# Second-layer gate as one ScalarE function, and every feed-forward low half on VectorE

## The chip, the cores and the metric

One Trainium2 chip, one core. The metric is the time of one execution on the device, in microseconds (us); lower is better. The engines are named as the profile names them: PE (TensorE matmul), PEld (TensorE weight load), DVE (VectorE), ACT (ScalarE), POOL (GpSimd), SP (SyncE, here only a DMA queue).

## What is computed

A clustered attention, a feed-forward layer with squared ReLU, and a second feed-forward layer whose gate is `h * sigmoid(1.702 h)`. All in float32, 1536 tokens, model width 512, inner width 2048.

```python
def _moe_ref(x, w_in, w_out):
    h = np.maximum(x @ w_in, 0.0)
    return (h * h @ w_out).astype(np.float32)

def _moe2_ref(x, w_in, w_out):
    h = x @ w_in
    g = h * (1.0 / (1.0 + np.exp(-1.702 * h)))
    return (g @ w_out).astype(np.float32)

x = attention(q, k, v, centroids)     # masked by cluster, then reshaped to (1536, 512)
x = _moe_ref(x, **moe)
return _moe2_ref(x, **moe2)
```

## The kernel before

**Halves.** Each float32 operand of the feed-forward matmuls is held as two numbers in the matmul type fp32r: a high half (ACT copies and rounds it) and a low half (the operand minus its high half). A product is three matmul passes, high x high, low x high and high x low (`PASSES`). So every weight and every activation needs one ACT copy and one subtraction, and the matmuls wait for both.

**Stages in time.** Attention runs to about 250 us. Then come four feed-forward stages. In the first layer's hidden part (L671) a unit is 12 matmuls, 48 units. In the first output part (L841) a unit is again 12 matmuls: 32 units for two of the three token blocks (c = 0, 1), then 16 for c = 2. In the second layer's hidden part the weights are taken in pairs j = 0 to 7 of inner blocks; by a Strassen-like scheme, a pair takes seven products (P1 to P7, L705, six matmuls each) and two plain ones in two pieces (Q0, Q0, Q1, Q1, L714), 11 x 6 = 66 matmuls. The second output part (L841) is as the first.

**What feeds PE.** `w_stages` makes a weight from its float64 words: `magnitude` (L207, ACT), `clamp` (L210), `shift` (L214), `join_low` (L218), `join_high` (L222), all DVE, then `high` (L226, ACT) and `low` (L229, POOL). `g_high` (L824, ACT) and `g_low` (L828, DVE) halve the activations for the output parts. For the second hidden part, DVE adds token blocks (`t_sum`, L857) and ACT and POOL halve them (`moving_high` L863, `moving_low` L867); DVE adds weight blocks (`sums_of`, four instructions at L805) and ACT and POOL halve the sums (L808, L811). DVE and ACT copy banks out (L850).

**The gate.** A product's bank is finished in three ways. `take` (L730, ACT) copies a partial sum to memory, and the next product adds onto the same bank, so PE must wait for the copy: P6 waits for the take behind P1, P7 for the one behind P6, P3 for the one behind P5. `plus` (L733, DVE) adds the stored partial sum to the bank. The gate of a bank is `gate_banked` (L718, ACT, sigmoid) and `times_banked` (L721, DVE, product); that of a stored sum is `gate_stored` (L724, ACT) and `times_stored` (L727, POOL). In the last pair the sum stays in a bank.

**Order.** Nothing is scheduled by the compiler. Each step is put into one list by `at(key, f)`, sorted by key and issued in that order; each engine runs its own in order, and an instruction that waits holds everything behind it on its engine. A weight's seven steps are 0.25 apart in key units (one unit is 12 matmuls).

## Time and profile before

| what | us |
| --- | --- |
| median of 3 runs | 782.68 (782.37 to 782.76) |
| the profiled execution: its time | 782.82 |
| the profiled execution: span of the core | 780.8 |
| PE busy | 762.9 of 780.8 |
| DVE, ACT, POOL busy | 516.9, 444.8, 275.7 |
| granted TensorE clock | 1.00 throughout |

Busy time of an engine is read stretch by stretch, since the stages have different limits. A PE row with a bracket, as `[0.92 <-ACT arena L730]`, says that PE stood idle for 0.92 us before it and what ended the wait. The duration in a row runs from the start of an instruction to its end, whatever it did in between. The slice line of the page shows PE at 9 tenths or more in every slice but the first and the last, which stand at 8.

### The profile page before, as it was taken

To read this page: it belongs to the slowest core of one execution; us is meant where nothing else is said; L and a number is where in the kernel's file an instruction comes from. 1 tells how busy PE (TensorE), PEld (TensorE's weight loads), DVE (VectorE), ACT (ScalarE), POOL (GpSimd) and SP (SyncE) were. 2 spreads that over 40 slices of the span, in tenths; PEclk is the share of its full clock that TensorE was granted. 3 is DMA by queue.
4 is the path that set the end of the run, shared out by engine and by line. 5 is a ranking of instruction groups with operands and counts; after the bars stand their busy time and mean duration, and the time that the engine had idled before them with its cause. 6 is when DMAs were issued, how large, how long until landed. Compare 5 with 4: busy or idle time off the path is not lost.

```text
span 780.8 us, 10718 instructions
## 1 busy us (share of the span) xinstructions
PE 762.9 (98%) x3899; PEld 597.5 (77%) x3899; DVE 516.9 (66%) x854; ACT 444.8 (57%) x823; POOL 275.7 (35%) x209
## 2 busy tenths in 40 slices
PE   8999999999999999999999999999999999999998
PEld 5676676777777788888888887788777778888886
DVE  6787877877876444444487249865888888777321
ACT  7877778778766566666644224454554555443321
POOL 3665664664501122122122005643655641222000
PEclk9999999999999999999999999999999999999999
DMA  5132322322220122223133000100211222221201
GB/s 183 42 102 63 90 74 61 89 74 55 52 87 25 58 95 94 101 88 109 55 108 109 1 27 1 55 27 28 82 54 55 81 82 82 85 104 55 107 1 55
DMA packets 18197, 54.54 MB, mean 70 GB/s; under 512 B 2720, under 2 KB 2976, under 8 KB 18144
## 3 DMA queue, kind: packets, MB, share of 16 engines
q1 hardware_dynamic: 17856, 53.32, 21.5%
q8 instruction: 31, 0.51, 0.2%
q10 hardware_dynamic: 288, 0.52, 0.2%
q14 instruction: 22, 0.18, 0.1%
HBM read 43.02 MB, written 3.15 MB: 59 GB/s over the span
## 4 chain that ended last, share of the span: by engine, by line
PE 77%; DVE 14%; ACT 5%; issue 2%; POOL 0%; DMA 0%; DVEq 0%; ACTq 0%; POOLq 0%
PE bank L841 30%; PE bank L671 15%; PE ps_v L576 8%; PE ps_p L558 7%; PE ps_s L533 4%; PE ps_s L536 4%; DVE arena L805 3%; PE bank L705 2%; DVE arena L210 2%; DVE arena L218 2%; PE ps_h L671 1%; ACT arena L550 1%; PE bank L714 1%; DVE arena L857 1%; DVE arena L542 1%
## 5 line engine op out<-in xcount | busy, mean ns | idle before, releaser
L841 PE MATMUL bank<-arena 128*128 128x512 f32 x1152 | 262.5, 389 | 1.6 <-DVE arena L828 1.6
L841 PEld LDWEIGHTS bank<-arena 128*128 128x128 f32 x1152 | 216.0, 188 | 47.7 <-DVE arena L828 2.9
L229 POOL TENSOR_TENSOR arena<-arena,arena 128x512 fp32r<-128x512 f32 x64 | 82.9, 1296 | 275.8 <-ACT arena L226 232.5
L828 DVE TENSOR_TENSOR arena<-arena,arena 128x512 fp32r<-128x512 f32 x96 | 80.0, 839 | 85.8 <-ACT arena L824 83.2
L671 PE MATMUL bank<-arena 128*128 128x512 f32 x528 | 119.8, 389 | 0.0
L824 ACT CAST arena<-arena 128x512 fp32r<-128x512 f32 x96 | 59.5, 621 | 99.4 <-PE bank L841 99.2
L671 PEld LDWEIGHTS bank<-arena 128*128 128x128 f32 x528 | 99.1, 188 | 20.5
L542 DVE TENSOR_SCALAR_CACHE_REDUCE arena<-ps_s 128x768 bf16<-128x768 f32 x96 | 91.8, 956 | 33.8 <-PE ps_s L536 25.2
L550 ACT ACTIVATE arena<-ps_s,arena 128x768 f32<-128x768 f32 x96 | 87.1, 907 | 37.5 <-DVE arena L542 37.2
L210 DVE TENSOR_SCALAR arena<-arena 128x512 f32<-128x512 f32 x64 | 46.3, 724 | 71.9 <-ACT arena L207 71.9
L705 PE MATMUL bank<-arena 128*128 128x512 f32 x336 | 82.0, 392 | 6.3 <-ACT arena L730 5.5
L226 ACT CAST arena<-arena 128x512 fp32r<-128x512 f32 x64 | 39.7, 620 | 77.2 <-DVE arena L222 77.2
L705 PEld LDWEIGHTS bank<-arena 128*128 128x128 f32 x336 | 62.5, 188 | 22.0 <-ACT arena L730 8.0
L576 PE MATMUL ps_v<-arena 128*64 128x384 f32 x384 | 72.1, 498 | 0.0
L558 PE MATMUL ps_p<-arena 128*128 128x128 f32 x576 | 70.8, 272 | 0.0
L558 PEld LDWEIGHTS ps_p<-arena 128*128 128x128 f32 x576 | 65.7, 141 | 2.3 <-issue 0.6
L533 PE MATMUL ps_s<-arena 128*128 128x384 f32 x192 | 54.7, 366 | 2.4 <-ACT arena L550 2.3
L536 PE MATMUL ps_s<-arena 80*128 80x384 f32 x192 | 49.9, 341 | 0.1
L218 DVE SCALAR_TENSOR_TENSOR arena<-arena 128x512 int32<-128x512 int32 x64 | 47.4, 740 | 1.8
L714 PE MATMUL bank<-arena 128*128 128x512 f32 x192 | 48.1, 389 | 0.0
L222 DVE SCALAR_TENSOR_TENSOR arena<-arena 128x512 int32<-128x512 int32 x64 | 46.2, 721 | 1.9
L566 DVE COPY arena<-ps_p 128x512 f32<-128x512 f32 x72 | 46.9, 677 | 0.0
(111 smaller groups left out, 910.3 us busy)
## 6 DMA issues: line engine op xcount, KB each, us to landing
arena<-in_w_dram SPq DMA_DIRECT2D x64, 512.0 KB, 3.2
arena<-arena SPq DMA_DIRECT2D x32, 192.0 KB, 2.5
arena<-in_k_t_dram SPq DMA_DIRECT2D x8, 384.0 KB, 3.8
arena<-in_v_dram SPq DMA_DIRECT2D x8, 384.0 KB, 3.3
out_dram<-arena SPq DMA_DIRECT2D x11, 256.0 KB, 2.1
arena<-in_q_t_dram SPq DMA_DIRECT2D x7, 384.0 KB, 3.4
arena<-arena SPq DMA_DIRECT2D x28, 48.0 KB, 2.1
arena<-in_q_t_dram ACTq DMA_DIRECT2D x1, 384.0 KB, 3.5
```

The lines of the kernel that those rows point to most:

```text
L218: nc.vector.scalar_tensor_tensor(out=x[0], in0=words[:, :, 0], scalar=29, in1=x[0], op0=ALU.logical_shift_right, op1=ALU.bitwise_or)
L229: nc.gpsimd.tensor_tensor(out=halves[:, 1, :], in0=x[0].bitcast(F32), in1=halves[:, 0, :].bitcast(F32), op=ALU.subtract)
L533: nc.tensor.matmul(ps[:, n, :HALF], lhsT=x_s[i][:, t * P:(t + 1) * P], rhs=k1_s[i][:, n * HALF:(n + 1) * HALF], start=True, stop=False)
L536: nc.tensor.matmul(ps[:, n, :HALF], lhsT=q2_s[i][:, t * P:(t + 1) * P], rhs=k2_s[i][:, n * HALF:(n + 1) * HALF], start=False, stop=True)
L542: nc.vector.tensor_scalar(out=unused, in0=s_t[g][:, :, :HALF], scalar1=-scale, scalar2=None, op0=ALU.mult, op1=ALU.min, accum_out=m_t[g])
L550: nc.scalar.activation(out=p_t[g].rearrange("p (n f) -> p n f", n=2), in_=s_t.pop(g)[:, :, :HALF], func=AF.Exp, bias=m_t.pop(g), scale=sca ...
L558: nc.tensor.transpose(ps[:, x * P:(x + 1) * P], p_t[2 * k + j][:, t * P:(t + 1) * P], ident)
L576: nc.tensor.matmul(pv_t[n][j * D:(j + 1) * D, :HALF], lhsT=raw[n // 2, "v"][:, j, t, :], rhs=pt_t[n, j][:, t, :], start=(t == 0), stop=(t ...
L671: nc.tensor.matmul(ps, lhsT=w[:, a, kk * P:(kk + 1) * P], rhs=xf[:, b, kk, c * CH:(c + 1) * CH], start=(n == 0), stop=(n == 3 * KD - 1))
L705: nc.tensor.matmul(ps, lhsT=w[:, a, off + x * P:off + (x + 1) * P], rhs=MOVING[moving][x][:, b, :], start=(n == 0 and name in ("P1", "P2", ...
L828: nc.vector.tensor_tensor(out=t[:, 1, :], in0=g_t[m][:, c, :], in1=t[:, 0, :].bitcast(F32), op=ALU.subtract)
L841: nc.tensor.matmul(ps, lhsT=lhsT, rhs=rhs, start=(m == 0 and e == 0), stop=(m == MF - 1 and e == 2))
```

## The change

The second layer's gate becomes one ACT instruction, the function `Gelu_apprx_sigmoid` (the argument times the sigmoid of 1.702 times it), written in place for stored sums and out of the bank for the others; the 27 products on DVE (L721) and the 21 on POOL (L727) are gone, and the last pair's sums go to memory as in the other pairs. The low halves of weights (62 of 64: those of the first layer's hidden blocks 0 and 1, made during attention, stay on POOL), of weight sums (16) and of token blocks (14) go from POOL to DVE. Keys are as before.

```diff
         def low():
-            nc.gpsimd.tensor_tensor(out=halves[:, 1, :], in0=x[0].bitcast(F32), in1=halves[:, 0, :].bitcast(F32),
-                                    op=ALU.subtract)
+            (nc.gpsimd if layer == 0 and which == 0 and m < 2 else nc.vector).tensor_tensor(
+                out=halves[:, 1, :], in0=x[0].bitcast(F32), in1=halves[:, 0, :].bitcast(F32), op=ALU.subtract)
...
-            def gate_banked(ps, g):
-                nc.scalar.activation(out=g, in_=ps, func=AF.Sigmoid, scale=1.702)
-
-            def times_banked(ps, g):
-                nc.vector.tensor_tensor(out=g, in0=ps, in1=g, op=ALU.mult)
-
-            def gate_stored(t, g):
-                nc.scalar.activation(out=t, in_=g, func=AF.Sigmoid, scale=1.702)
-
-            def times_stored(t, g):
-                nc.gpsimd.tensor_tensor(out=g, in0=g, in1=t, op=ALU.mult)
+            def gate(x, g):
+
+                nc.scalar.activation(out=g, in_=x, func=AF.Gelu_apprx_sigmoid)
...
                     for name, ps, g in (("P2", c12, g00), ("P7", u_, g11), ("P3", c2x, g01)):
-                        if last:
...
-                        else:
-                            t = g_t[MF - 2 + gates[0] // 3 % 2][:, gates[0] % 3, :]
-                            gates[0] += 1
-                            after(name, j, 0.12, on(plus, ps, g, g))
-                            after(name, j, 0.7, gate_stored, t, g)
-                            after(name, j, 1.2, times_stored, t, g)
-                    after("P4", j, 0.1, on(gate_banked, u_, g10))
-                    after("P4", j, 0.6, on(times_banked, u_, g10))
+                        after(name, j, 0.12, on(plus, ps, g, g))
+                        after(name, j, 0.7, gate, g, g)
+                    after("P4", j, 0.1, on(gate, u_, g10))
...
                 def split_low(to, of):
-                    nc.gpsimd.tensor_tensor(out=to[:, 1, :], in0=of, in1=to[:, 0, :].bitcast(F32), op=ALU.subtract)
+                    nc.vector.tensor_tensor(out=to[:, 1, :], in0=of, in1=to[:, 0, :].bitcast(F32), op=ALU.subtract)
...
             def moving_low(name, x):
                 t = MOVING[name][x]
-                nc.gpsimd.tensor_tensor(out=t[:, 1, :], in0=moving_whole(name, x), in1=t[:, 0, :].bitcast(F32), op=ALU.subtract)
+                nc.vector.tensor_tensor(out=t[:, 1, :], in0=moving_whole(name, x), in1=t[:, 0, :].bitcast(F32), op=ALU.subtract)
```

In the changed file the lines behind the gate have moved: `plus` L733 is L725, `take` L730 is L722, the gate is L719, `sums_of` L805 and L811 are L781 and L787, `g_low` L828 is L804, `t_sum` L857 is L833, `moving_low` L867 is L843. The order of PE's and of ACT's instructions is otherwise unchanged (one gate stands where one sigmoid stood, and one table load before the first of them, as before); POOL's queue ends with attention's last step and the two lows that it keeps.

DVE in the second layer's hidden part, one middle pair, before: behind the two sums of one pair (banks 2632 and 2636) come the four weight sums, two products of gates, then a weight, a sum, a product, a weight.

```order
L733 TENSOR_TENSOR arena_59<-bank_2632,arena_59 128x512
L733 TENSOR_TENSOR arena_59<-bank_2636,arena_59 128x512
L805 TENSOR_TENSOR arena_59<-arena_59 128x256 x4
L721 TENSOR_TENSOR arena_59<-bank_2639,arena_59 128x512
L721 TENSOR_TENSOR arena_59<-bank_2632,arena_59 128x512
L210 TENSOR_SCALAR arena_59<-arena_59 128x512
L214 TENSOR_SCALAR arena_59<-arena_59 128x512
L218 SCALAR_TENSOR_TENSOR arena_59<-arena_59 128x512
L222 SCALAR_TENSOR_TENSOR arena_59<-arena_59 128x512
L733 TENSOR_TENSOR arena_59<-bank_2635,arena_59 128x512
L721 TENSOR_TENSOR arena_59<-bank_2638,arena_59 128x512
L210 TENSOR_SCALAR arena_59<-arena_59 128x512
```

The same place in the changed kernel:

```order
L725 TENSOR_TENSOR arena_59<-bank_2632,arena_59 128x512
L725 TENSOR_TENSOR arena_59<-bank_2636,arena_59 128x512
L781 TENSOR_TENSOR arena_59<-arena_59 128x256 x4
L787 TENSOR_TENSOR arena_58<-arena_59,arena_58 128x512
L210 TENSOR_SCALAR arena_59<-arena_59 128x512
L787 TENSOR_TENSOR arena_58<-arena_59,arena_58 128x512
L214 TENSOR_SCALAR arena_59<-arena_59 128x512
L218 SCALAR_TENSOR_TENSOR arena_59<-arena_59 128x512
L222 SCALAR_TENSOR_TENSOR arena_59<-arena_59 128x512
L725 TENSOR_TENSOR arena_59<-bank_2635,arena_59 128x512
L229 TENSOR_TENSOR arena_58<-arena_59,arena_58 128x512
L210 TENSOR_SCALAR arena_59<-arena_59 128x512
```

The products (L721) are gone; the two lows of the weight sums (L787) stand behind the sums, and each weight's low (L229) stands behind its L222.

DVE at the end of the first output part, where the third token block is multiplied and the token sums are made, before:

```order
L857 TENSOR_TENSOR arena_59<-arena_59 128x512 x2
L828 TENSOR_TENSOR arena_58<-arena_59,arena_58 128x512
L857 TENSOR_TENSOR arena_59<-arena_59 128x512 x5
L828 TENSOR_TENSOR arena_58<-arena_59,arena_58 128x512
L857 TENSOR_TENSOR arena_59<-arena_59 128x512
L828 TENSOR_TENSOR arena_58<-arena_59,arena_58 128x512
```

The same place in the changed kernel, from just behind the first two `moving_low`:

```order
L833 TENSOR_TENSOR arena_59<-arena_59 128x512 x2
L804 TENSOR_TENSOR arena_58<-arena_59,arena_58 128x512
L833 TENSOR_TENSOR arena_59<-arena_59 128x512
L843 TENSOR_TENSOR arena_58<-arena_59,arena_58 128x512
L833 TENSOR_TENSOR arena_59<-arena_59 128x512 x2
L843 TENSOR_TENSOR arena_58<-arena_59,arena_58 128x512
L833 TENSOR_TENSOR arena_59<-arena_59 128x512 x2
L804 TENSOR_TENSOR arena_58<-arena_59,arena_58 128x512
L833 TENSOR_TENSOR arena_59<-arena_59 128x512
L843 TENSOR_TENSOR arena_58<-arena_59,arena_58 128x512
L804 TENSOR_TENSOR arena_58<-arena_59,arena_58 128x512
```

Between the low halves that PE waits for (L804) now stand the lows of token blocks (L843), which were POOL's.

## Rows read from the trace of the kernel before

**Rows 1.** The page's first part: busy us, share of the span, instructions.

```profile
PE 762.9 (98%) x3899; PEld 597.5 (77%) x3899; DVE 516.9 (66%) x854; ACT 444.8 (57%) x823; POOL 275.7 (35%) x209
```

**Rows 2.** Busy time by stretch (us; start:end, length, engines, then PEclk, DMA, GB/s).

```profile
249.80:385.20 135.40, 135.40 (x605) 110.30 (x605) 59.81 (x97) 83.06 (x144) 29.75 (x23) 1.00 0.26 90
...
472.20:518.10 45.90, 44.30 (x193) 35.68 (x192) 37.50 (x37) 20.83 (x37) 27.82 (x18) 1.00 0.07 23
518.10:646.20 128.10, 121.84 (x530) 98.55 (x530) 102.83 (x142) 66.86 (x119) 66.29 (x50) 1.00 0.18 62
646.20:776.80 130.60, 130.60 (x577) 107.93 (x575) 73.87 (x111) 48.63 (x82) 18.15 (x14) 1.00 0.19 66
...
574.40:590.56 16.16, 15.25 (x66) 12.31 (x66) 14.09 (x19) 8.24 (x16) 9.23 (x8) 1.00 0.18 60
```

**Rows 3.** The chain that ended last: start us, us, what.

```profile
385.19 87.05 PE bank L841 x384
```

**Rows 4.** PE in time: start us, us, what, idle before it and its releaser.

```profile
484.54 8.48 PE L841 MATMUL bank<-arena 128*128 128x512 f32 x36 [0.97 <-DVE arena L828]
...
518.14 8.32 PE L705 MATMUL bank<-arena 128*128 128x512 f32 x36
...
575.03 3.01 PE L705 MATMUL bank<-arena 128*128 128x512 f32 x12 [0.92 <-ACT arena L730]
...
591.19 3.02 PE L705 MATMUL bank<-arena 128*128 128x512 f32 x12 [0.91 <-ACT arena L730]
...
644.66 1.67 PE L705 MATMUL bank<-arena 128*128 128x512 f32 x6 [0.76 <-DVE bank L733]
646.17 1.09 PE L841 MATMUL bank<-arena 128*128 128x512 f32 x4
```

**Rows 5.** DVE, POOL and ACT in time, in one pair of the second hidden part.

```profile
578.77 4.51 DVE L805 TENSOR_TENSOR arena<-arena 128x256 f32<-128x256 f32 x4
...
579.64 2.90 POOL L727 TENSOR_TENSOR arena<-arena 128x512 f32<-128x512 f32 x2
...
583.61 2.55 POOL L811 TENSOR_TENSOR arena<-arena,arena 128x512 fp32r<-128x512 f32 x2 [1.07 <-ACT arena L808]
...
585.08 1.36 DVE L210 TENSOR_SCALAR arena<-arena 128x512 f32<-128x512 f32 x1 [0.39 <-ACT arena L207]
...
588.39 0.62 ACT L226 CAST arena<-arena 128x512 fp32r<-128x512 f32 x1 [2.87 <-DVE arena L222]
...
590.56 1.07 ACT L730 COPY arena<-bank 128x512 f32<-128x512 f32 x2
```

**Rows 6.** Instructions grouped by line and form: count, busy us, mean ns, idle before.

```profile
L229 POOL TENSOR_TENSOR arena<-arena,arena 128x512 fp32r<-128x512 f32 x64 | 82.9, 1296 | 275.8 <-ACT arena L226 232.5 <-PE bank L671 25.1 <-issue 18.2
...
L721 DVE TENSOR_TENSOR arena<-bank,arena 128x512 f32<-128x512 f32 x27 | 18.5, 689 | 15.6 <-ACT arena L718 14.9
...
L724 ACT ACTIVATE arena<-arena 128x512 f32<-128x512 f32 x21 | 13.1, 633 | 5.2 <-DVE arena L733 5.1
```

**Rows 7.** In time: three kinds of DVE instruction at moments when POOL stands still.

```profile
551.52 0.42 DVE L210 TENSOR_SCALAR arena<-arena 128x512 f32<-128x512 f32 x1
...
551.86 0.42 DVE L805 TENSOR_TENSOR arena<-arena 128x256 f32<-128x256 f32 x1
...
650.54 1.28 DVE L828 TENSOR_TENSOR arena<-arena,arena 128x512 fp32r<-128x512 f32 x2
```

**Rows 8.** DVE in time, the token sums up to a low half that PE waits for.

```profile
473.48 3.48 DVE L857 TENSOR_TENSOR arena<-arena 128x512 f32<-128x512 f32 x2
...
478.59 5.29 DVE L857 TENSOR_TENSOR arena<-arena 128x512 f32<-128x512 f32 x5
...
483.80 0.68 DVE L828 TENSOR_TENSOR arena<-arena,arena 128x512 fp32r<-128x512 f32 x1
```

**Rows 9.** POOL and DVE in time, one weight of the second output part.

```profile
666.23 1.30 POOL L229 TENSOR_TENSOR arena<-arena,arena 128x512 fp32r<-128x512 f32 x1 [3.61 <-ACT arena L226]
...
666.70 1.37 DVE L828 TENSOR_TENSOR arena<-arena,arena 128x512 fp32r<-128x512 f32 x1 [1.21 <-ACT arena L824]
```

More of the change, by code (lines that the diff above doesn't have):

```diff
@@ L733, in plus @@
                 nc.vector.tensor_tensor(out=out, in0=ps, in1=g, op=ALU.add)
-            gates = [0]
             def second_hidden(u0):
@@ L759, in second_hidden @@
                     m = 2 * j
-                    last = j == MJ - 1
                     def on(f, which, g, *more):
@@ L772, in second_hidden @@
                     for name, ps, g in (("P2", c12, g00), ("P7", u_, g11), ("P3", c2x, g01)):
-                        if last:
-                            def to_bank(ps=ps, name=name):
-                                return banks[6] if name == "P7" else sum_banks(ps[1])[ps[0]]
-                            after(name, j, 0.12, lambda ps=ps, g=g, to=to_bank: plus(sum_banks(ps[1])[ps[0]], g, to()))
-                            after(name, j, 0.7, lambda g=g, to=to_bank: gate_banked(to(), g))
-                            after(name, j, 1.2, lambda g=g, to=to_bank: times_banked(to(), g))
-                        else:
-                            t = g_t[MF - 2 + gates[0] // 3 % 2][:, gates[0] % 3, :]
-                            gates[0] += 1
-                            after(name, j, 0.12, on(plus, ps, g, g))
-                            after(name, j, 0.7, gate_stored, t, g)
-                            after(name, j, 1.2, times_stored, t, g)
-                    after("P4", j, 0.1, on(gate_banked, u_, g10))
-                    after("P4", j, 0.6, on(times_banked, u_, g10))
+                        after(name, j, 0.12, on(plus, ps, g, g))
+                        after(name, j, 0.7, gate, g, g)
+                    after("P4", j, 0.1, on(gate, u_, g10))
                     for i in range(2):
                         g = g_t[m + i][:, 2, :]
-                        after(f"Q{i}", j, 0.1, lambda i=i, g=g: gate_banked(banks[6 + i], g))
-                        after(f"Q{i}", j, 0.6, lambda i=i, g=g: times_banked(banks[6 + i], g))
+                        after(f"Q{i}", j, 0.1, lambda i=i, g=g: gate(banks[6 + i], g))
                 return order, done
```

## The prediction, made before the changed kernel ran

> **What bounds the kernel now.** I read the busy line first: PE is busy 762.9 of 780.8 us [rows 1]. Then the stretches: in the first layer's hidden part and in the last output part PE is busy without a gap (135.40 of 135.40, 130.60 of 130.60); in the stretch from 472.20 to 518.10 and in the second layer's hidden part (518.10 to 646.20) it is not, and just there DVE is busy 37.50 of 45.90 and 102.83 of 128.10 and POOL 27.82 and 66.29 [rows 2]. So the change can win only what PE loses in these two stretches, and can lose wherever DVE has no room left.
>
> How much PE loses is worked out from its pace, since a gap also costs a refill that the idle time in the brackets leaves out. Undisturbed, 384 matmuls take 87.05 us, 0.2267 each [rows 3]. The first output part has 576 and begins at 385.19; it should end at 515.77, and the next part begins at 518.14: 2.37 us lost [rows 3, 4], in three gaps, of which the first is shown (0.97, PE waits for a low half, L828). The second hidden part has 528: 119.70 us by the pace, 128.03 measured (518.14 to 646.17), 8.33 lost [rows 4], in seven gaps, 1.19 each. One pair shows it: 575.03 to 591.19 is 16.16 for 66 matmuls, which need 14.96, so 1.20 is lost where the bracket says 0.91. Six of the seven wait for a `take` (L730), the last for a `plus` (L733). The sum of all is **10.7 us**.
>
> **Why the take is late.** Follow one pair backward [rows 5]. The take of 590.56 stands on ACT behind a weight's high half (L226 at 588.39), which had waited 2.87 us for the weight's DVE steps. These stood behind L210 at 585.08, which took 1.36, and that behind the four weight sums at 578.77, which took 4.51. The same instructions take 0.42 each when POOL is still [rows 7]: the four sums could take 1.7, L210 0.42. What runs beside them is POOL: products 579.64 to 582.54 beside the sums, lows from 583.61 to 586.16 beside L210 [rows 5]. So POOL's work of 1.30 an instruction [rows 6] is not free: while it reads, a DVE instruction with both inputs in memory stands still. L721, with one input in a bank, shows a mean of 689 ns over all 27 and no stretching [rows 6].
>
> **The change part by part.** The profiled execution is taken at its own time, 782.82 (span 780.8 and 2.0 around it); it stands 0.14 above the median of 782.68, so the answer is the median less what is won.
>
> *Products.* 27 L721 of 0.689 leave DVE, 21 of POOL's go, and the gate stays one ACT instruction: 633 ns is the price of the sigmoid [rows 6]. The new function is not in the trace; ACT's other rows of this width bound it, 0.54 for a copy (L730, two in 1.07) and 0.62 for L226 [rows 5], so the kind of function hardly shows in them, and I take the sigmoid's 0.63. At twice that, six gates a pair would add 3.8 to ACT's 8.24 [rows 2], still under 14.96. The built order has one table load before the first gate, as before.
>
> *Lows.* 92 subtractions go to DVE. The nearest row is L828, of the same form: two in 1.28, 0.64 each with POOL still [rows 7]; the other end is its 1.37 beside POOL [rows 9], which no longer applies once POOL is empty. I take 0.64.
>
> *DVE in a pair*, before 14.09 of 16.16 [rows 2]: take off 2.8 for the sums, 0.94 for L210, 2.07 for three products; add four lows, 2.56: 10.8. Each low also makes DVE wait for ACT's high half (0.62 [rows 5]) if nothing stands between; four times that is 2.5. The total is 13.3 of the 14.96 that PE needs: it fits.
>
> *The take.* Behind the sums now stand one or two lows (0.64 each) in place of the two products: the sums end 2.8 earlier, L210 is 0.94 shorter, and the lows cost at most 1.28, so the high half and the take behind it come at least 2.5 earlier. PE lost 1.20. All four regular gaps go, with 1.3 to spare. The low L229 behind L222 stands in front of the next `plus`, but by then DVE is 2.5 ahead.
>
> *Edge gaps.* The first gap of the seven and that before P6 of the last pair have the same chain and about 0.5 to 1 to spare, since more lows stand in front. The last (0.76, at 644.66) waits for a `plus` behind a weight's low, an output low and L210; I count about 0.6 to spare. In the stretch from 472.20, the low half that PE waited for began at 483.80, after eight DVE instructions from 473.48 on, 10.3 us [rows 8]. Now twelve stand there (four lows of token blocks more): at 0.64 to 0.70 they take 7.7 to 8.4, so it comes 1.9 to 2.6 earlier; PE lost about 1.25 there. The other two gaps are shorter and behind the same queue. All ten go, the edges with less than a microsecond to spare.
>
> *Covers.* In the first layer's hidden part DVE is busy 59.81 of 135.40 [rows 2], and some twenty lows of 0.64 with their waits lie beside PE. In the last output part DVE is busy 73.87 of 130.60; there L828 sat idle for 1.21 waiting for ACT's L824, then took 1.37 beside POOL's low [rows 9]. The low now stands in that idle time, as ACT makes the weight's high half just before L824, and L828 is back at 0.64: not later than before. If that cover were gone, one weight in 5.2 us would cost DVE 0.64 and 0.62 more, and three buffers of halves let a low half come two units (24 matmuls, 5.4 us) after its buffer is free, some 4 us more than the two instructions need.
>
> Sum: 782.68 - 2.37 - 8.33 = **772.0**. I forecast 772.1.
>
> **A rule that speaks against it.** DVE is the fullest engine beside PE in the pairs (14.09 of 16.16), while POOL is at 9.23 [rows 2]. The Trainium skill (Perfetto Trace Analysis, Optimizing Scalar/DVE Operations) says that a saturated DVE may be helped by offloading work to ScalarE or even GpSimd, which is the reverse of this change; the same paragraph warns that moving work between DVE and GpSimd might not help, as they share an SBUF read port. By the first half the time is the slower rival's below, by the second the forecast's; the rows with DVE instructions at three times their length beside POOL are for the second. The Trainium skill (SBUF — State Buffer, Who interferes with whom) makes it sharper: a DVE instruction with two SBUF inputs contends with a GpSimd one that reads, and the later one blocks fully. The L805 and L828 rows agree; L210, with one input, is stretched too, which that page gives to a two-port mode.
>
> **Rivals.**
>
> *The edges stay (0.22).* The regular gaps go, 4 x 1.20 = 4.8, and the six with little to spare stay, since a wait for ACT's high half is longer than 0.62 where ACT itself waits for PE: 782.7 - 4.8 = **777.9**. For it: DVE now waits for ACT 92 times more, in order. Against: ACT is busy 8.24 of 16.16 [rows 2].
>
> *Slower, DVE becomes the bound (0.06).* If the stretched rows are not POOL's doing, a pair costs DVE 14.09 - 2.07 + 2.56 + 2.5 = 17.1 against 16.16, 0.9 more in each of eight pairs, 7; and the stretch from 472.20 gets 18 lows more, 37.50 + 11.5 = 49.0 against 45.90, 3.1: **792.8**. It decides from the point at which a pair's DVE work with its waits is over 16.16. Against: every stretched row here lies beside a POOL row, and the same instruction is short where POOL is still.
>
> *No change (0.06).* The take is late by ACT's own order and not by DVE: then the gaps stay, **782.7**. Against: ACT waits 2.87 for DVE just ahead of it [rows 5].
>
> **How the numbers follow.** All gaps gone 0.66, edges stay 0.22, no change 0.06, slower 0.06. The range goes from 771.2 (the sum less the spread of the runs, 0.4, and as much for reading the pace) to 777.9, which takes in the second case: 0.88 by these chances, so no more than it needs. A measurement tells about 0.2% (1.6 us) from no change; faster 0.88, same 0.06, slower 0.06.
>
> **What would show it.** PE in the second hidden part without gaps, 528 matmuls in about 119.7 us and a pair in 14.96; the four weight sums at about 1.8, L210 at 0.42 throughout; DVE's busy time lower in the pairs although 92 instructions came to it; lows at 0.64 to 0.70. Wrong, if DVE's L210 or sums stay stretched with POOL empty, if a PE row still waits for a `take`, if the gate takes more than 0.65, or if a gap appears in the output parts.

## The result and the profile after

| | median, us | of all runs, us |
| --- | --- | --- |
| before, in the same comparison | 782.52 | 782.36 to 782.76, 4 runs |
| changed | 771.31 | 771.12 to 771.58, 4 runs |

The ratio is 0.9857, with a 95% interval of 0.9840 to 0.9874: faster by 11.2 us. The profiled execution took 771.23 us with a span of 769.5, against 780.8 before.

In the changed file the output matmuls, L841 before, are L817; `w_stages` keeps its lines. Where an experiment adds lines, the text says what its line is.

The page of the changed kernel, its busy line:

```profile
PE 759.8 (99%) x3899; PEld 598.3 (78%) x3899; DVE 498.2 (65%) x919; ACT 446.9 (58%) x823; POOL 123.2 (16%) x96
```

DVE has 65 instructions more than before and is busy 18.7 us less [rows 1]. By their own durations, 27 products gone (18.6) and 92 low halves come (63.5) would have made it 45 more. Group by group, the DVE instructions that both kernels have are some 61 us shorter after the change: that much of DVE's busy time before was no work of its own, though the page counted it as such.

Busy time by stretch, after (start:end, length, then PE, PEld, DVE, ACT, POOL, clock, DMA share, GB/s), to be laid beside [rows 2]. The last row is a stretch of one pair's length:

```profile
472.20:515.80 43.60, 43.60 (x194) 36.13 (x193) 32.81 (x56) 21.28 (x38) 0.00 (x0) 1.00 0.07 25
515.80:635.50 119.70, 119.70 (x530) 99.15 (x529) 82.81 (x149) 69.47 (x120) 0.00 (x0) 1.00 0.19 66
...
556.20:571.16 14.96, 14.96 (x67) 12.39 (x67) 10.66 (x20) 8.67 (x15) 0.00 (x0) 1.00 0.22 79
```

PE is busy for the whole of both stretches in which it lost time before, and POOL for none of them. In a pair DVE went from 14.09 of 16.16 us to 10.66 of 14.96.

The chain that ended last (start us, us, what), the pieces with which its last three stages begin:

```profile
384.82 130.56 PE bank L817 x576
...
515.38 8.16 PE bank L705 x36
...
635.07 130.57 PE bank L817 x576
```

The same view of the kernel before, the pieces that answer to the last two:

```profile
518.30 8.16 PE bank L705 x36
...
646.34 130.64 PE bank L841 x576
```

Stage by stage this is where the 11.3 us of span went. The first output part took 133.11 (518.30 less the 385.19 of [rows 3]) and takes 130.56: 2.55. The second hidden part took 128.04 and takes 119.69: 8.35. The last output part is 0.07 shorter, and 0.37 was there when the first output part began (385.19 against 384.82), ahead of every stage for which the change was reckoned to matter. These 0.37 are scatter and not a gain: in the kernels below that leave the attention as it is, this part begins anywhere from 384.80 to 385.42. What lies behind the last matmul is 0.04 longer.

One pair in time, after: DVE, ACT and PE, to be read beside [rows 5]:

```profile
581.88 0.43 DVE L210 TENSOR_SCALAR arena<-arena 128x512 f32<-128x512 f32 x1 [1.15 <-ACT arena L207]
582.06 0.59 ACT L722 COPY arena<-bank 128x512 f32<-128x512 f32 x1 [0.21 <-PE bank L705]
...
583.22 1.52 PE L714 MATMUL bank<-arena 128*128 128x512 f32 x6
...
584.25 0.62 ACT L226 CAST arena<-arena 128x512 fp32r<-128x512 f32 x1 [0.24 <-DVE arena L222]
584.58 2.88 PE L705 MATMUL bank<-arena 128*128 128x512 f32 x12
...
588.11 1.80 DVE L781 TENSOR_TENSOR arena<-arena 128x256 f32<-128x256 f32 x4
```

The four weight sums take 1.80 where they took 4.51, and L210 0.43 where it took 1.36. ACT waits 0.24 for a weight's DVE steps where it waited 2.87. And the bracket of the `take` (582.06) has turned round: it waits for PE, and the matmuls that need it (584.58) start without a bracket.

The groups of the changed kernel by line and form (count, busy us, mean ns, idle before and its releasers):

```profile
L229 DVE TENSOR_TENSOR arena<-arena,arena 128x512 fp32r<-128x512 f32 x62 | 42.9, 691 | 43.9 <-ACT arena L226 43.0
...
L210 DVE TENSOR_SCALAR arena<-arena 128x512 f32<-128x512 f32 x64 | 27.1, 423 | 43.2 <-ACT arena L207 43.2
...
L719 ACT ACTIVATE arena<-arena 128x512 f32<-128x512 f32 x24 | 15.2, 633 | 20.8 <-DVE arena L725 20.6
```

A low half is 0.69 on DVE where it was 1.30 on POOL, and the fused gate from memory costs 633 ns, exactly what the sigmoid alone cost [rows 6].

### The profile page after: what moved, and what is told of

Its sections match the earlier page's. It is cut to its first block, busy times and chain, and to the rows that moved or that the text cites. A ratio compares the mean times of both kernels' runs of the same rounds, so it can differ in the third digit from the quotient of the medians.

```text
span 769.5 us, 10549 instructions
## 1 busy us (share of the span) xinstructions
PE 759.8 (99%) x3899; PEld 598.3 (78%) x3899; DVE 498.2 (65%) x919; ACT 446.9 (58%) x823; POOL 123.2 (16%) x96
## 4 chain that ended last, share of the span: by engine, by line
PE 93%; ACT 3%; DVE 3%; issue 0%; DMA 0%; POOL 0%; DVEq 0%; ACTq 0%; POOLq 0%
PE bank L817 34%; PE bank L671 16%; PE bank L705 10%; PE ps_v L576 8%; PE ps_p L558 7%; PE bank L714 6%; PE ps_s L533 5%; PE ps_s L536 4%; PE ps_h L671 1%; ACT arena L550 1%; PE ps_aff L394 1%; DVE arena L542 1%; PE ps_r L593 1%; PE ps_back L411 1%; PE ps_oh L477 1%; PE ps_aff L397 0%
## 5 line engine op out<-in xcount | busy, mean ns | idle before, releaser
L817 PE MATMUL bank<-arena 128*128 128x512 f32 x1152 | 261.4, 389 | 0.0
L817 PEld LDWEIGHTS bank<-arena 128*128 128x128 f32 x1152 | 216.3, 188 | 44.8
L804 DVE TENSOR_TENSOR arena<-arena,arena 128x512 fp32r<-128x512 f32 x96 | 66.2, 690 | 82.0 <-ACT arena L800 79.8
L542 DVE TENSOR_SCALAR_CACHE_REDUCE arena<-ps_s 128x768 bf16<-128x768 f32 x96 | 91.7, 955 | 33.7 <-PE ps_s L536 25.1
L550 ACT ACTIVATE arena<-ps_s,arena 128x768 f32<-128x768 f32 x96 | 87.1, 907 | 37.3 <-DVE arena L542 37.0
L705 PE MATMUL bank<-arena 128*128 128x512 f32 x336 | 80.9, 389 | 0.0
L705 PEld LDWEIGHTS bank<-arena 128*128 128x128 f32 x336 | 63.1, 188 | 13.1
L229 DVE TENSOR_TENSOR arena<-arena,arena 128x512 fp32r<-128x512 f32 x62 | 42.9, 691 | 43.9 <-ACT arena L226 43.0
L210 DVE TENSOR_SCALAR arena<-arena 128x512 f32<-128x512 f32 x64 | 27.1, 423 | 43.2 <-ACT arena L207 43.2
L676 ACT ACTIVATE arena<-bank 128x512 f32<-128x512 f32 x44 | 26.2, 596 | 37.5 <-PE bank L671 37.5
L533 PEld LDWEIGHTS ps_s<-arena 128*128 128x128 f32 x192 | 31.2, 189 | 19.9 <-issue 8.5
```

What stands on the lines that cost most here:

```text
L533: nc.tensor.matmul(ps[:, n, :HALF], lhsT=x_s[i][:, t * P:(t + 1) * P], rhs=k1_s[i][:, n * HALF:(n + 1) * HALF], start=True, stop=False)
L542: nc.vector.tensor_scalar(out=unused, in0=s_t[g][:, :, :HALF], scalar1=-scale, scalar2=None, op0=ALU.mult, op1=ALU.min, accum_out=m_t[g])
L550: nc.scalar.activation(out=p_t[g].rearrange("p (n f) -> p n f", n=2), in_=s_t.pop(g)[:, :, :HALF], func=AF.Exp, bias=m_t.pop(g), scale=sca ...
L705: nc.tensor.matmul(ps, lhsT=w[:, a, off + x * P:off + (x + 1) * P], rhs=MOVING[moving][x][:, b, :], start=(n == 0 and name in ("P1", "P2", ...
L804: nc.vector.tensor_tensor(out=t[:, 1, :], in0=g_t[m][:, c, :], in1=t[:, 0, :].bitcast(F32), op=ALU.subtract)
L817: nc.tensor.matmul(ps, lhsT=lhsT, rhs=rhs, start=(m == 0 and e == 0), stop=(m == MF - 1 and e == 2))
```

## The experiments

All times are medians of four runs; the kernel before, run beside them, had medians of 782.39 to 782.77. Each ratio is against the kernel before on the same chip.

| kernel | us | ratio to before, 95% interval |
| --- | --- | --- |
| lows only | 776.97 | 0.9928 (0.9913 to 0.9943) |
| gate only | 774.73 | 0.9899 (0.9884 to 0.9913) |
| changed, POOL reads beside | 786.47 | 1.0051 (1.0034 to 1.0067) |
| changed, POOL writes beside | 771.83 | 0.9863 (0.9848 to 0.9877) |
| changed, token lows back | 773.66 | 0.9888 (0.9873 to 0.9902) |
| changed, weight and sum lows back | 771.89 | 0.9866 (0.9851 to 0.9880) |
| changed, lows twice | 776.71 | 0.9926 (0.9911 to 0.9941) |
| two-step gate, all products and lows on DVE | 773.21 | 0.9883 (0.9867 to 0.9900) |
| changed, POOL reads a spare buffer | 777.29 | 0.9933 (0.9917 to 0.9950) |
| changed, first weight spread out | 770.58 | 0.9846 (0.9831 to 0.9861) |

The theory is that of the prediction: POOL's reading makes DVE stand still, which makes a `take` or a low half late for PE. Its rivals: the new gate's smaller count of instructions is what counts; or DVE's room; or buffers that POOL holds.

### The lows alone

The gate of before, and the three kinds of low half on DVE:

```diff
-            nc.gpsimd.tensor_tensor(out=halves[:, 1, :], in0=x[0].bitcast(F32), in1=halves[:, 0, :].bitcast(F32),
+            (nc.gpsimd if layer == 0 and which == 0 and m < 2 else nc.vector).tensor_tensor(
...
-                    nc.gpsimd.tensor_tensor(out=to[:, 1, :], in0=of, in1=to[:, 0, :].bitcast(F32), op=ALU.subtract)
+                    nc.vector.tensor_tensor(out=to[:, 1, :], in0=of, in1=to[:, 0, :].bitcast(F32), op=ALU.subtract)
...
-                nc.gpsimd.tensor_tensor(out=t[:, 1, :], in0=moving_whole(name, x), in1=t[:, 0, :].bitcast(F32), op=ALU.subtract)
+                nc.vector.tensor_tensor(out=t[:, 1, :], in0=moving_whole(name, x), in1=t[:, 0, :].bitcast(F32), op=ALU.subtract)
```

> The kernel before, with all low halves on DVE as in the change, but with its own gate: sigmoid on ACT, 27 products on DVE, 21 on POOL. My theory: the gaps come from DVE instructions that stand still beside POOL's reads, on the chain that ends in the take. The three gaps at the end of the first output part go (2.4 us). In the pairs the products of POOL still lie beside the four weight sums, the DVE products stay in front, and two lows are added: the take is as late as before or later, so the gaps there stay or grow: 780 to 785 us, DVE's weight sums still near 1 us each. The rival, that it is enough to empty DVE's neighbour of the lows: 772 to 776.

Measured: 776.97 us, 5.7 less than before: outside the time that I had expected, and 1 above the rival's. PE's rows with a bracket in time, two of the six that are left (L730 is the `take`, L705 the matmuls):

```profile
586.30 3.01 PE L705 MATMUL bank<-arena 128*128 128x512 f32 x12 [0.55 <-ACT arena L730]
602.05 3.06 PE L705 MATMUL bank<-arena 128*128 128x512 f32 x12 [0.50 <-ACT arena L730]
```

And the weight sums and L210 in its groups:

```profile
L210 DVE TENSOR_SCALAR arena<-arena 128x512 f32<-128x512 f32 x64 | 27.6, 431 | 29.8 <-ACT arena L207 29.8
...
L805 DVE TENSOR_TENSOR arena<-arena 128x256 f32<-128x256 f32 x32 | 24.7, 772 | 0.8
```

There is no bracket in the first output part any more. The second hidden part takes 124.26 (PE in time, 515.75 to 640.01) where it took 128.03; a pair takes 15.75 (602.05 less 586.30) in place of 16.16. L210 is clean without POOL's lows; the sums, beside POOL's products, are still long. I had expected the two lows that now stand between sums and L210 to eat the gain. A working after the fact, from means of the whole kernel: sums 983 to 772 in the mean, four times, 0.84; L210 0.94; two lows at 0.64, 1.28 lost; net 0.50 earlier, and the pair gained 0.41.

### The gate alone

The new gate, and all low halves back on POOL (the three edits above turned round).

> The changed kernel with all low halves back on POOL: only the gate is one ACT function. My theory: in the pairs the weight sums lose their stretch (POOL's products lay there), two DVE products are gone, so the take comes some 3 us earlier and the 8.3 us of the pairs are won, although POOL still does four lows a pair; the 2.4 us at the end of the first output part stay: 774 to 775 us. The rival, that it takes both halves of the change: 777 to 780.

Measured: 774.73, 7.9 less than before, as expected. PE's bracketed rows behind 470 us, all there are:

```profile
484.25 8.48 PE L817 MATMUL bank<-arena 128*128 128x512 f32 x36 [0.97 <-DVE arena L804]
...
492.95 5.76 PE L817 MATMUL bank<-arena 128*128 128x512 f32 x24 [0.22 <-DVE arena L804]
...
499.12 18.90 PE L817 MATMUL bank<-arena 128*128 128x512 f32 x82 [0.41 <-DVE arena L804]
```

The second hidden part has no gap, though L210 still shows a mean of 657 ns beside POOL's lows; the three gaps of the first output part stand as before. So the gate cures the pairs by itself, and the lows cure the end of the first output part. The two single gains add up to 13.6, 2.4 more than both together: roughly the part of the pairs' loss that either of them removes.

### Which lows

The token blocks' lows alone go back to POOL:

```diff
-                nc.vector.tensor_tensor(out=t[:, 1, :], in0=moving_whole(name, x), in1=t[:, 0, :].bitcast(F32), op=ALU.subtract)
+                nc.gpsimd.tensor_tensor(out=t[:, 1, :], in0=moving_whole(name, x), in1=t[:, 0, :].bitcast(F32), op=ALU.subtract)
```

> The changed kernel with one part undone: the fourteen low halves of token blocks (moving_low) go back to GpSimd; the low halves of weights and of sums and the new gate stay as changed. My theory: it is the token blocks' lows, 1.64 us each when GpSimd makes them beside DVE, that stretch the t_sum instructions in front of the low half for which TensorE waits at the end of the first output part, so the three gaps there come back and nothing else: 773.4 to 774.3 us, with the second hidden part still without a gap. The rival: any one kind of low is too little to make TensorE wait, and only all three together do: 771.2 to 771.8.

Measured: 773.66. PE's bracketed rows behind 470 us:

```profile
484.20 13.94 PE L817 MATMUL bank<-arena 128*128 128x512 f32 x60 [0.97 <-DVE arena L804]
498.40 18.89 PE L817 MATMUL bank<-arena 128*128 128x512 f32 x82 [0.26 <-DVE arena L804]
```

Two of the three brackets are back, the largest unchanged, and nothing in the pairs: 2.35 us for fourteen instructions, as expected, of which the first output part shows 1.86 (132.42 against 130.56). The eight token sums take 1365 ns in the mean again, where they take 681 in the changed kernel, and DVE waits for nothing between them: no buffer that POOL holds is in play there, only the length of DVE's own instructions.

The other 78, of weights and of weight sums, go back instead:

```diff
-            (nc.gpsimd if layer == 0 and which == 0 and m < 2 else nc.vector).tensor_tensor(
+            nc.gpsimd.tensor_tensor(
...
-                    nc.vector.tensor_tensor(out=to[:, 1, :], in0=of, in1=to[:, 0, :].bitcast(F32), op=ALU.subtract)
+                    nc.gpsimd.tensor_tensor(out=to[:, 1, :], in0=of, in1=to[:, 0, :].bitcast(F32), op=ALU.subtract)
```

> The changed kernel with the other part undone: the low halves of weights and of weight sums go back to GpSimd, the token blocks' low halves and the new gate stay as changed. My theory: with the new gate the take has spare time, so stretched weight sums reach no TensorE wait, and moving these 78 lows was worth nothing: 771.2 to 772.0 us, although DVE's weight sums and L210 are stretched again. The rival: a part of the gain at the edges of the second hidden part hangs on these lows too, and gaps come back there: 773 to 776.

Measured: 771.89. Its chain, and a group:

```profile
384.80 130.56 PE bank L817 x576
635.04 130.57 PE bank L817 x576
```

```profile
L210 DVE TENSOR_SCALAR arena<-arena 128x512 f32<-128x512 f32 x64 | 40.9, 639 | 95.6 <-ACT arena L207 95.6
```

PE runs as in the changed kernel to within 0.03 us up to its last matmul. L210 is stretched again by half its length and nobody is late for it. The 0.6 us between the two times lies behind the last matmul (the spans are 770.0 and 769.5). With the fused gate in place, these 78 moves are worth nothing on PE's path; what the 0.6 behind it comes from no run shows.

### Emptying POOL, or giving DVE room

The gate of before in two instructions, but with every product and every low half on DVE; against the kernel with the lows alone, one word:

```diff
             def times_stored(t, g):
-                nc.gpsimd.tensor_tensor(out=g, in0=g, in1=t, op=ALU.mult)
+                nc.vector.tensor_tensor(out=g, in0=g, in1=t, op=ALU.mult)
```

> The kernel before, but with all low halves on DVE and with all 48 products of argument and sigmoid on DVE as well: the gate stays two instructions, and GpSimd is as empty as in the changed kernel. It separates the two things that the new gate does, to empty GpSimd and to take 48 products of 0.69 us (33 us) off the path. The first theory, that GpSimd's reads alone made the takes late: nearly all of the gain stays, 771.5 to 774 us. The second, that DVE must also have room: DVE would be busy 82.8 + 33.1 = 115.9 of 119.7 us in the second hidden part before its waits for ScalarE, gaps come back there, and the time is 780 to 800. I hold the second for likelier.

Measured: 773.21. I held the wrong one of the two for likelier. Busy time in one pair, and PE's only bracketed row behind 470 us (L733 is the `plus`):

```profile
555.69:570.74 15.05, 15.05 (x68) 12.45 (x67) 13.90 (x26) 8.25 (x15) 0.00 (x0) 1.00 0.21 71
```

```profile
634.86 1.66 PE L705 MATMUL bank<-arena 128*128 128x512 f32 x6 [0.84 <-DVE bank L733]
```

DVE is busy 13.90 of 15.05 us, a larger share than before the change (14.09 of 16.16 [rows 2]), and yet this pair takes just 0.09 more than PE's 14.96, and the three behind it 0.09 to 0.21 more. With POOL empty a nearly full DVE costs 1.9 us in all, the largest piece at one edge; with POOL reading, a DVE of the same busy time cost 8.35 in this part alone. Against the kernel with the lows alone, only the engine of 21 products differs: DVE has more to do, its weight sums go from 772 to 422 ns in the mean, no `take` is late any more, and the time falls by 3.8. So of the gate's two effects, with the lows on DVE, the emptying of POOL is worth 3.8 and the 48 products saved 1.9.

### How much room DVE has left

Each of the 92 moved lows is computed twice on DVE:

```diff
+            if layer or which or m >= 2:
+                nc.vector.tensor_tensor(out=halves[:, 1, :], in0=x[0].bitcast(F32), in1=halves[:, 0, :].bitcast(F32), op=ALU.subtract)
...
+                    nc.vector.tensor_tensor(out=to[:, 1, :], in0=of, in1=to[:, 0, :].bitcast(F32), op=ALU.subtract)
...
+                nc.vector.tensor_tensor(out=t[:, 1, :], in0=moving_whole(name, x), in1=t[:, 0, :].bitcast(F32), op=ALU.subtract)
```

> The changed kernel, and each low half that was moved is computed twice in a row on DVE (the second writes the same numbers to the same place): 92 more instructions of 0.69 us on DVE, none on GpSimd. It measures how far DVE is from being the bound. DVE is busy 82.8 of 119.7 us in the second hidden part now, and some 50 of the added instructions (35 us) fall there: about 118 of 119.7 without its waits. My theory: the room is used up and gaps come back, both there and at the end of the first output part: 775 to 790 us. The rival: most of DVE's idle time is waiting that the added work fills, and the buffers take up the rest: 771.3 to 773.

Measured: 776.71, within the first range. PE's bracketed rows in the first output part (L807 is `g_low`), and a pair's busy time:

```profile
484.25 8.49 PE L820 MATMUL bank<-arena 128*128 128x512 f32 x36 [0.79 <-DVE arena L807]
493.96 14.02 PE L820 MATMUL bank<-arena 128*128 128x512 f32 x60 [1.22 <-DVE arena L807]
508.65 10.73 PE L820 MATMUL bank<-arena 128*128 128x512 f32 x46 [0.67 <-DVE arena L807]
```

```profile
589.59:604.63 15.04, 15.04 (x68) 12.43 (x67) 13.24 (x23) 8.26 (x15) 0.00 (x0) 1.00 0.23 71
```

The pairs nearly fit, at 15.04 with 13.24 busy; the second hidden part has two short brackets (0.17 at 563.07, 0.25 at 638.67, both for a `plus`) and takes 1.3 more than in the changed kernel (120.97 against 119.69). The larger loss, 3.7 (134.29 against 130.56), is at the end of the first output part, where token sums and lows come in a burst: it needs no average of DVE to be full there.

### Reading or writing, and whose data

Three kernels add useless work on POOL to the changed kernel, next to each of the 92 moved lows. In the first, POOL computes the same difference once more into a spare buffer, in two halves of 256 columns:

```diff
+            if layer or which or m >= 2:
+                nc.gpsimd.tensor_tensor(out=spare, in0=x[0].bitcast(F32)[:, 0*256:0*256+256], in1=halves[:, 0, :].bitcast(F32)[:, 0*256:0*256+256], op=ALU.subtract)
+                nc.gpsimd.tensor_tensor(out=spare, in0=x[0].bitcast(F32)[:, 1*256:1*256+256], in1=halves[:, 0, :].bitcast(F32)[:, 1*256:1*256+256], op=ALU.subtract)
...
```

> The changed kernel, and beside each of the 92 moved lows POOL computes the same difference once more into a spare buffer that nobody reads (two instructions of half the width). My theory, that DVE stands still while POOL reads: DVE instructions are stretched again to two or three times their length although DVE has the same work as in the changed kernel, DVE's busy time grows by 30 us or more in the feed-forward stages, and some of the gaps return: 773 to 778 us. The rival, that POOL's work cost nothing but its own lateness: 771.3, no stretched row.

Measured: 786.47, slower than the kernel before and far above the 773 to 778 expected, though not one instruction of DVE, ACT or PE was added. Its groups (L812 is `g_low`, L213 what is L210 otherwise), the largest of its gaps, and DVE ahead of it, from the first token lows (L851) to the low half (L812) that PE waits for:

```profile
L812 DVE TENSOR_TENSOR arena<-arena,arena 128x512 fp32r<-128x512 f32 x96 | 81.6, 855 | 58.8 <-ACT arena L808 56.8 <-PE bank L825 2.0
...
L213 DVE TENSOR_SCALAR arena<-arena 128x512 f32<-128x512 f32 x64 | 45.6, 713 | 35.0 <-ACT arena L210 35.0
```

```profile
488.16 15.53 PE L825 MATMUL bank<-arena 128*128 128x512 f32 x60 [4.37 <-DVE arena L812]
```

```profile
473.71 2.37 DVE L851 TENSOR_TENSOR arena<-arena,arena 128x512 fp32r<-128x512 f32 x2
...
487.43 0.68 DVE L812 TENSOR_TENSOR arena<-arena,arena 128x512 fp32r<-128x512 f32 x1
```

The twelve instructions ahead of the low half take 13.72 us where they take 7.23 in the changed kernel, and DVE waits for nothing between them: this gap comes of the stretching alone. The first output part loses 8.0 in all. A part of that is the clock: behind PE's idle 4.37 us the granted clock was 0.50 from 490 to 492 us, the lower of its two levels (1.2 GHz; 1.00 is 2.4 GHz), and the 60 matmuls of this row took 15.53 where 60 took 13.94 in the kernel with the token lows back. The second hidden part loses 5.2; `take` brackets are back there (0.69, 0.31 and 0.33), and the last `plus` is 1.60 late.

POOL's reads also hold the buffers that they read. No wait of another engine in the feed-forward part of the trace is put down to them, but a wait is put down only to what came last. Two more kernels take that away. In one POOL only writes, four fills of 256 columns for each low, released by a one-column fill on DVE:

```diff
+                nc.vector.memset(spare[:, 0:1], 0.0)
+                nc.gpsimd.memset(spare, 0.0)
+                nc.gpsimd.memset(spare, 0.0)
+                nc.gpsimd.memset(spare, 0.0)
+                nc.gpsimd.memset(spare, 0.0)
```

> As the run with the spare differences, but POOL only fills the spare buffer (four fills of 256 columns at each low, released by a one-column DVE fill), and reads nothing. If only POOL's reading holds DVE: 771.3 to 771.8 and no stretched row (the one-column fills cost DVE 0.1 us each). If any work of POOL in memory holds it: stretched rows and 773 to 778, as with the differences.

Measured: 771.83, no gap of PE. Its groups (L818 is `g_low`, L213 the former L210):

```profile
L818 DVE TENSOR_TENSOR arena<-arena,arena 128x512 fp32r<-128x512 f32 x96 | 66.3, 691 | 79.7 <-ACT arena L814 77.5 <-PE bank L831 2.0
...
L213 DVE TENSOR_SCALAR arena<-arena 128x512 f32<-128x512 f32 x64 | 29.9, 467 | 43.1 <-ACT arena L210 42.4 <-ACT arena L731 0.3 <-DVE arena L796 0.3
```

DVE's two-input instructions keep their length beside a POOL that only writes. The one-input L213 is longer by 44 ns in the mean.

In the other POOL reads, but only a spare buffer of its own, released in the same way (224 columns, as two spare buffers of that size are what the memory has room for):

```diff
+                nc.vector.memset(spare[:, 0:1], 0.0)
+                nc.gpsimd.tensor_tensor(out=spare, in0=still, in1=still, op=ALU.subtract)
+                nc.gpsimd.tensor_tensor(out=spare, in0=still, in1=still, op=ALU.subtract)
```

> The changed kernel, and for each moved low half GpSimd does two subtractions of a spare 128x224 buffer from itself into another spare buffer; nothing of the kernel's own data is read, and no buffer of the kernel waits for GpSimd. A one-column fill on DVE releases them. In the run with reads of the kernel's own data the buffers that GpSimd read also came free later, so its loss holds two causes; here only the reading is left. My theory, that GpSimd's reading itself makes DVE stand still: DVE's two-input instructions are stretched as there (t_sum and the lows over 0.80 us in the mean, against 0.69), gaps of TensorE come back at the end of the first output part, and the time is 773 to 782 us. The rival, that the loss there came from buffers held longer: 771.3 to 772.3, as with fills alone.

Measured: 777.29, 6.0 more than the changed kernel. PE's bracketed rows behind 470 us, and DVE and POOL in time (L845 is `t_sum`, L816 `g_low`, L237 a one-column fill, the rows of POOL its reads):

```profile
484.60 8.48 PE L829 MATMUL bank<-arena 128*128 128x512 f32 x36 [1.28 <-DVE arena L816]
494.33 14.49 PE L829 MATMUL bank<-arena 128*128 128x512 f32 x60 [1.26 <-DVE arena L816]
510.15 10.74 PE L829 MATMUL bank<-arena 128*128 128x512 f32 x46 [1.33 <-DVE arena L816]
```

```profile
475.63 0.69 DVE L845 TENSOR_TENSOR arena<-arena 128x512 f32<-128x512 f32 x1 [1.10 <-issue]
...
482.10 0.93 POOL L857 TENSOR_TENSOR spare<-still 128x224 f32<-128x224 f32 x1 [0.65 <-DVE spare L856]
482.53 1.04 DVE L845 TENSOR_TENSOR arena<-arena 128x512 f32<-128x512 f32 x1
...
483.11 0.89 POOL L858 TENSOR_TENSOR spare<-still 128x224 f32<-128x224 f32 x1
...
483.50 1.04 DVE L816 TENSOR_TENSOR arena<-arena,arena 128x512 fp32r<-128x512 f32 x1
...
493.54 0.06 DVE L237 MEMSET spare<- 128x1 f32 x1 [1.12 <-POOL spare L858]
493.58 0.69 DVE L816 TENSOR_TENSOR arena<-arena,arena 128x512 fp32r<-128x512 f32 x1
...
577.59 0.56 POOL L238 TENSOR_TENSOR spare<-still 128x224 f32<-128x224 f32 x1 [3.68 <-DVE spare L237]
```

POOL reads nothing of the kernel's own here, and the same DVE instruction is 0.69 where POOL's last read has ended (475.63) and 1.04 where one is under way (482.53); POOL's own read, 0.56 where DVE is not in its way (the last row), takes 0.89 and 0.93 there. In the mean the token sums are 818 ns and the token lows 865, as expected; the output lows are 723, less than expected. So reading by itself is enough for the stretching. The three gaps are back, in the same place and for the same low half, but not by the stretching alone: the one-column fills write POOL's spare buffer, and DVE stands in front of them until POOL's last read is done. Ahead of the first gap DVE is idle for 1.10 (475.63), where the kernel with fills has 0.93 in the same place; that this wait too is such a fill's is my reading of the order. Five instructions are longer by some 0.35, and the low half comes 3.0 later than in the changed kernel, counted from the part's first matmul. Ahead of the second and of the third gap a fill waits 1.12 just before the low half (0.79 in the kernel with fills). The waits of the kernel with fills cost PE nothing; what they add here is not separated.

That the reading makes PE wait with no such fill in between is shown by the first kernel and by the token lows back on POOL. Of the first kernel's 15.2 us, 6.0 come back with reads of a spare buffer (of seven eighths of the width), 5.4 of them in the first output part and 0.3 in the second hidden part. The other 9.2 hold the fall of the clock (about 1.6, by the 60 matmuls above); held buffers and the larger reads are the rest, which no run here separates.

### A version beyond the change

Behind the start, and some short gaps inside the attention, the changed kernel has two gaps left, at the attention's end:

```profile
232.41 0.62 PE L533 MATMUL ps_s<-arena 128*128 128x384 f32 x2 [0.30 <-ACT arena L550]
233.78 0.62 PE L533 MATMUL ps_s<-arena 128*128 128x384 f32 x2 [0.40 <-ACT arena L550]
```

The seven steps that prepare the first layer's first weight stand there in a row, in front of L542 (DVE) and L550 (ACT). They were begun earlier and spread:

```diff
-                weights(layer, which, m, first)
+                weights(layer, which, m, *((-16.5, 0.8) if (layer, which, m) == (0, 0, 0) else (first,)))
```

> The changed kernel, with the preparation of the first layer's first weight begun earlier and its seven steps spread out (0.8 of a unit apart in place of 0.25), so that no five of them stand in a row on DVE and ScalarE among the attention's instructions. The last two gaps of TensorE behind the start, 0.30 and 0.40 us at 232.41 and 233.78, both wait for the attention's exponentials (L550), which stand behind those steps. My theory: these two gaps go, and with the refill behind each the time falls by 0.7 to 1.3 us, to 770.0 to 770.7. The rival: spread out, the same steps hold up other exponentials as much: 771.0 to 771.7.

Measured: 770.58 (770.32 to 770.81). Both gaps are gone; the first output part begins 0.91 earlier than in the changed kernel and has its full pace:

```profile
383.91 130.56 PE bank L817 x576
```

It is the fastest of all the kernels here. Against the changed kernel's 771.31 the 0.7 is less than a comparison of times can tell; that it is there rests on the trace.

## Why the prediction was right

**The sum.** It said that PE lost 2.37 and 8.33 us in two stretches, all in ten gaps, and that all ten go: 772.0, told as 772.1. The stretches gave 2.55 and 8.35. The first was mis-sized by a slip in the reading: its start was taken from the chain (385.19) and its end from PE in time (518.14), and the two views are 0.16 apart, since a matmul's own row begins before the one ahead of it has ended; the chain has 518.30. Of the 0.8 that the result lies lower than the forecast, 0.16 is the lower median of the kernel before in the second comparison, 0.2 these two stretches, 0.4 the start and the end of the feed-forward part, and 0.1 was rounded up; that is 0.1 too much, as the profiled spans differ by 11.3 and the medians by 11.2. The start, 0.37, is luck: the sum has no term for it, and it is no larger than the scatter of that start. The time lies 0.1 above the bottom of the range, so on that side the range was barely wide enough. Working the loss out from PE's pace, and not from the brackets, was what made the sum fit: the pace says 1.20 a pair, the bracket 0.91 [rows 4].

**Why the take was late.** Shown for the pairs by the rows and by two kernels. The sums are 1.80, L210 is 0.42 throughout, and the `take` now waits for PE. Reckoned from the matmuls in front of it, it began 1.80 behind their start before (590.56 [rows 5], where those matmuls have this row in the trace of before):

```profile
588.76 1.52 PE L714 MATMUL bank<-arena 128*128 128x512 f32 x6
```

It now begins 1.16 ahead of them (582.06 against 583.22): 2.96 earlier, where the prediction had said at least 2.5. That POOL's products did it is shown by the two kernels that differ in their engine alone (776.97 and 773.21). That it is POOL's reading is shown for the length of DVE's instructions (reads against fills). For the `take` it is supported by the first kernel with reads, in which `take` brackets come back, but there held buffers are not excluded; reads of the spare buffer left the pairs without a gap. The rival of no change, a take that is late by ACT's own order, falls with the same rows: ACT's order is the same and the take now waits for PE.

**DVE in a pair.** Predicted 10.8, measured 10.66. **The waits** of 2.5 on top were over-sized: in the kernel with all the products on DVE, whose pairs DVE itself paces, only 1.15 of 15.05 is left idle, so no more than that was waiting that other work could not fill.

**Costs.** The gate at 0.63 was right (633 ns, 594 from a bank). The low at 0.64: 0.69 as a duration, but 0.60 from one start to the next where nothing waits. That is why the low half that PE waited for came earlier than reckoned. These are DVE's rows in the changed kernel, from the first token lows (L843) to that low half (L804):

```profile
473.11 1.28 DVE L843 TENSOR_TENSOR arena<-arena,arena 128x512 fp32r<-128x512 f32 x2
...
480.34 0.68 DVE L804 TENSOR_TENSOR arena<-arena,arena 128x512 fp32r<-128x512 f32 x1
```

Twelve instructions stand there, as foreseen, and take 7.23 us, where 7.7 to 8.4 was said; the low half began at 483.80 before [rows 8] and begins at 480.34, 3.1 earlier if the 0.37 of the start is left out (said: 1.9 to 2.6).

**The edges** were called near ("less than a microsecond to spare") and given 0.22 to stay. None stayed, and with the new gate they were not that near: with the weights' and sums' lows back on POOL, L210 is 639 ns in the mean and still no edge shows a gap.

**Which part does what** was left open by the prediction, and the runs say it: the gate frees the pairs, fourteen token lows free the first output part, and with the new gate the other 78 lows do nothing for the time.

**The slower rival** asked for a DVE that stays stretched with POOL empty. No run shows that. Even a DVE that is busy 13.90 us a pair leaves the pair at 15.05 to 15.17, a long way from the 16.16 at which that rival would have begun to lose.

**The rule weighed.** The Trainium skill (Perfetto Trace Analysis, Optimizing Scalar/DVE Operations) lets a saturated DVE give work to other engines, GpSimd among them, and warns that between these two it might not help. Here the warning decides: all 48 products and all the moved lows on DVE gave 773.21, against 782.39 for the kernel before beside it, in which POOL had 21 and 92 of them. The Trainium skill (SBUF — State Buffer, Who interferes with whom) sets apart a GpSimd instruction that reads from one that only writes: two-input DVE instructions are to be held by the first alone, one-input ones in a two-port mode by GpSimd whatever it does. The runs agree: in the mean 691 ns with fills and 855 with reads for the first kind, 467 and 713 for the second, from 690 and 423. Which mode the one-input ones ran in no row shows. The Trainium skill (SBUF — State Buffer, Summary: rules for kernel authors) says, too, that the later one of two waits for the whole of the earlier. The rows of the spare-buffer reads fit it, though both engines' are lengthened: the DVE row at 482.53 starts within POOL's of 482.10, and POOL's at 483.11 within that DVE row, so each is in its turn the later one.

## What to carry to other kernels

Where two engines hinder each other, the busy share of the one holds its waiting for the other: look for rows of one line with two durations, and lay the other engine's rows beside the long ones, before calling an engine full. Give the work back to the faster engine where the other one's reads fall beside a queue that somebody waits for; where nobody waits, as for 78 of 92 instructions here once the gate was changed, the move is free and worth nothing. And reckon a loss from the bound engine's undisturbed pace, since the idle time in front of its instructions left out a quarter of it here.

## What was not expected of the hardware

- DVE's two-input instructions and POOL's reads of 224 columns lengthened each other about alike, by some 0.35 us on either side, with no data in common.
- After PE had stood idle for 4.37 us in one kernel, its granted clock was 0.50 from 490 to 492 us and 1.00 again from 494 on; so a single late low half cost more than its bracket.
- Fills on POOL are not quite free either: DVE's L213 and L217, with one input, went from 423 and 426 to 467 and 463 ns in the mean, while everything with two inputs kept its length.
- A DVE that is busy 13.90 of 15.05 us still let PE finish a pair in 15.05 to 15.17, where it needs 14.96. An engine that takes its work in order, 92% full and with waits among it, was hardly a bound here.
